# q in PSUM for the attention of a gated layer, GpSimd's sums let run, weight parts handed out by pieces

## The chip, the cores and the metric

The kernel runs on one core of a Trainium2 chip. The metric is the device time of one execution in microseconds. Three runs of the kernel before gave 785.12, 785.23 and 786.01; the median is 785.23.

## The reference

All inputs are float32: S = 2048 positions, D = 640 channels, 32 heads of 20 channels, F = 1536.

```python
xn = _layernorm(x)
# s: attention of each position over 8 earlier ones, 2 apart
qkv = xn @ wqkv                    # D x 3D, split into q, k, v and 32 heads of 20
idx = pos[:, None] - arange(8) * 2 # W, dil = 8, 2
logits = einsum("bhsd,bhswd->bhsw", q, k[idx]) * 20 ** -0.5   # idx < 0: -1e9
o = einsum("bhsw,bhswd->bhsd", softmax(logits), v[idx])
s = o.reshape(B, S, D) @ wo
# g: a gated feed-forward
h = (xn @ w_gate) * (xn @ w_up)    # D x F each
return x + s * silu(h @ w_down)
```

## The kernel before

Every product runs on TensorE as three products of split numbers: each operand is cut into a high part (ScalarE copies it to float32r) and a low part (the rest, subtracted on VectorE or GpSimd), and high x high, high x low and low x high are added up in one PSUM bank (`mm3`, L96). The low part of the weights enters only with the last third of a product.

The program is one long list of instructions. Each engine works through its own list in order, so the order in which the code issues them is the schedule. The stages are:

- layer norm, transposition and the first products (to about 76 us);
- the stage of the units. The attention is cut into 12 units: 6 groups of 5 or 6 heads (`GROUPS`), each for the even and the odd positions. A unit needs 8 `qkv` products (L365); units from the second group on go through a scratch in DRAM and are read back with `load_kq` and `load_kv`. After every two units come two *pieces* `gate_up(f, ch)` (L528): the product of 128 columns of the gate weights, then of the up weights, with 512 positions, 15 matmuls each. ScalarE copies the gate result out of PSUM (`gs`, L539), and VectorE multiplies it with the up result, straight from PSUM (`hs`, L550). That multiplication is put off (`finish_piece`) until the next piece or a later place;
- the rest of the pieces, from 327 us to 565 us; at the end of it the output projection is prepared;
- the output projection in pairs of rows (`pair_product`, L918) and singly, and then the down projection (`product`, L787), both by a scheme with seven products for eight, to the end.

The attention itself is a Python generator (`attention`, L396). `qkv` loops and pieces call `advance` with a budget, and the generator issues VectorE work until the costs it yields have used up the budget. For each unit it goes over four pairs of window places: VectorE multiplies q, read twice, with k shifted (`t`, L445), sums over the 20 channels (`lg`, L463), and in between does the previous unit's values: e times v into one of two buffers (`t` or, for place 0, `o`, L425), which GpSimd adds to `o` (L427). The softmax follows, with the exponential on ScalarE (L485). The e of a unit lies in PSUM.

GpSimd's list is ordered by hand too. A one-element copy of `t` (`behind`, L153) ahead of the sums makes GpSimd wait for the q·k multiplication:

```python
nc.vector.tensor_mul(t, q, k)
if late or beside:
    behind(t[:, 0, :1])
if late:
    late.pop()()
if beside:
    beside.pop(0)[1]()
```

`beside` holds the low parts of the next block of gate and up weights (L143): three subtractions for each block f from 3 to 10, put there by `split_wf_beside(f + 1)` after the block's first piece. What is left of them is issued by `all_beside(f)` ahead of block f's first piece.

PSUM has eight banks: three turn for the tag q (qkv products and most others), two each for g and u (gate and up), one is e.

Of the kernel before, what the change touches and what calls it, by code (L numbers as in the profile page):

```python
# [19 lines left out]
P = 128  # L20
# [7 lines left out]
CH = 512  # L28
# [23 lines left out]
def kernel(  # L52
# [23 lines left out]
    def st(shape, tag, bufs, dt=F32):  # L76
        cnt[0] += 1
        return sb.tile(shape, dt, tag=tag, bufs=bufs, name=f"{tag}_{cnt[0]}")

    def pt(shape, tag, bufs):  # L80
        cnt[0] += 1
        return ps.tile(shape, F32, tag=tag, bufs=bufs, name=f"{tag}_{cnt[0]}")

# [14 lines left out]
    def skip(n):  # L98

        cnt[0] += 1  # L100
        sb.tile([P, n // 4], F32, tag=f"skip_{cnt[0]}", bufs=1, name=f"skip_{cnt[0]}")
# [40 lines left out]
            k = slice(k0, min(k0 + 2, KD))  # L142
            beside.append((f, lambda k=k: nc.gpsimd.tensor_sub(lo[:, k], raw[:, k], hi[:, k].bitcast(F32))))  # L143

    def some_beside(t):

        if beside:
            behind(t[:, 0, :1])
            beside.pop(0)[1]()

    def behind(y):

        nc.gpsimd.tensor_copy(no_wait[0], y)  # L153
# [14 lines left out]
    def load_x(s, n, t, cuts=(0, D)):  # L168
# [3 lines left out]
        for i in range(n):  # L172
            xt[s + i] = t[:, i, :]

    skip(128)
    xa, xe = st([P, 3, D], "t", 2), st([P, 3, D], "t", 2)
    load_x(0, 1, xa[:, 0:1], (0, HALF, D))
# [218 lines left out]
    def attention():  # L396

        def flat(y):
            return y.rearrange("p i c -> p (i c)")

        twice = st([P, 2, NE * CMAX], "t", 2)
        terms = st([P, 2, NE * CMAX], "t", 2)
        weights = pt([P, CH], "e", 1)
        places = NE * W
        m_ps = weights[0:1, CH - places:].rearrange("p (i w) -> p i w", w=W)
        nc.vector.tensor_copy(m_ps, mask)
        before, late, loaded = None, [], set(range(DIL))

        def ahead(n, parts):

            if n < len(ORDER) and ORDER[n] in made:
                for a in parts:
                    if (n, a) not in loaded and ORDER[n] >= DIL:
                        loaded.add((n, a))
                        (load_kq if a == 0 else lambda u: load_kv(u, 1))(ORDER[n])

        def values(w):

            u, e, o = before
            nh = GROUPS[UN[u][0]]  # L420
            c = nh * DH
            y = flat(o)
            t = terms[:, w % 2, :NE * c] if w else y
            v = flat(kv_t[u][:, 1, w:w + NE, :]).rearrange("p (n d) -> p n d", d=DH)
            nc.vector.tensor_mul(t.rearrange("p (n d) -> p n d", d=DH),  # L425
                                 e[:, :, w].unsqueeze(2).to_broadcast([P, NE * nh, DH]), v)
            return NE * c * 1.3e-3, lambda: nc.gpsimd.tensor_add(y, y, t)  # L427

        for n, u in enumerate(ORDER + [None]):
            if u is not None:  # L430
                while u not in made:
                    yield None
                ahead(n, (0, 1))
                g, r = UN[u]
                nh = GROUPS[g]
                c = nh * DH
                q, kv = flat(q_t[u]).unsqueeze(1).to_broadcast([P, 2, NE * c]), kv_t[u]
                lg = st([P, NE * nh, W], "lg", 2)
                t = twice.rearrange("p a c -> p (a c)")[:, :2 * NE * c].rearrange("p (a c) -> p a c", a=2)
            for j in PAIRS:  # L440
                if u is not None:
                    ahead(n + 1, (0,))
                    k = flat(kv[:, 0, j:j + NE, :])
                    k = bass.AP(k.tensor, k.offset, [k.ap[0], [c, 2], k.ap[1]])
                    nc.vector.tensor_mul(t, q, k)  # L445
                    if late or beside:
                        behind(t[:, 0, :1])
                    if late:
                        late.pop()()
                    if beside:  # L450
                        beside.pop(0)[1]()
                    yield 2 * NE * c * 1.22e-3
                elif late:
                    late.pop()()
                if before is not None:
                    cost, add = values(j or 1)
                    if j:
                        add()
                    else:
                        late.append(add)  # L460
                    yield cost
                if u is not None:
                    nc.vector.tensor_reduce(out=lg[:, :, j:j + 2].rearrange("p n a -> p a n"),  # L463
                                            in_=t.rearrange("p a (n d) -> p a n d", d=DH), op=ALU.add, axis=AX.X)
                    yield 2 * NE * c * 1.2e-3
                if before is not None:
                    cost, add = values(j + 1 if j else 0)
                    if j:
                        late.append(add)
                    yield cost  # L470
            if late:
                late.pop()()
            if u is None:
                store_o(before)
                return
            ahead(n + 1, (0, 1))
            m0 = lg[0:1].rearrange("p (i h) w -> p i h w", h=nh)
            nc.vector.tensor_add(m0, m0, m_ps.unsqueeze(2).to_broadcast([1, NE, nh, W]))
            e = weights[:, :NE * nh * W].rearrange("p (n w) -> p n w", w=W)
            most = weights[:, CH - places - NE * nh:CH - places]  # L480
            sm = st([P, 2, NE * nh], "sm", 2)
            nc.vector.tensor_reduce(out=most, in_=lg, op=ALU.max, axis=AX.X)
            nc.vector.tensor_sub(lg, lg, most.unsqueeze(2).to_broadcast([P, NE * nh, W]))
            yield 1.5
            nc.scalar.activation(e, lg, AF.Exp, scale=SCALE)  # L485
            finish_piece()
            yield 0.5
            nc.vector.tensor_reduce(out=sm[:, 0, :], in_=e, op=ALU.add, axis=AX.X)
            nc.vector.reciprocal(sm[:, 1, :], sm[:, 0, :])
            nc.vector.tensor_mul(e, e, sm[:, 1, :].unsqueeze(2).to_broadcast([P, NE * nh, W]))  # L490
            if before is not None:
                store_o(before)
            before = u, e, st([P, NE, c], "o", 1)
            yield 1.3

    def store_o(unit):

        u, _, o = unit
        g, r = UN[u]
        c = GROUPS[g] * DH  # L500
        for b in range(NQ):
            c0, c1 = max(GOFF[g], b * QC), min(GOFF[g] + c, (b + 1) * QC)
            if c0 < c1:
                nc.sync.dma_start(o_scr[r, b, :, :, c0 - b * QC:c1 - b * QC].rearrange("s p c -> p s c"),
                                  o[:, :, c0 - GOFF[g]:c1 - GOFF[g]])
# [3 lines left out]
    def advance(budget):  # L509
        credit[0] += budget  # L510
        while running and credit[0] > 0:
            cost = next(running[0], 0)
            if cost == 0:
                running.pop()
            elif cost is None:
                break
            else:
                credit[0] -= cost
        if credit[0] > 0:
            credit[0] = 0  # L520
# [4 lines left out]
    def gate_up_half(f, ch, n, p, c=slice(0, CH), **parts):  # L525
        mm3(p[:, c], [([t[:, k, n, :] for t in wf[f]], [t[:, k, c] for t in xT[ch]]) for k in range(KD)], **parts)

    def gate_up(f, ch, between=(), amid=(), part=None):  # L528
        if part is None:
            pp = [pt([P, CH], "g", 2), pt([P, CH], "u", 2)]  # L530
            c = slice(0, CH)
        else:
            pp, c = part, slice(CH // 2, CH)
        last = (f, ch) == (KF - 1, NCH - 1)
        gate_up_half(f, ch, 0, pp[0], c)
        for act in amid:
            act()
        gs = st([P, CH], "gs", 2)
        nc.scalar.activation(gs, pp[0], AF.Copy)  # L539
        for act in between:  # L540
            act()
        share = (c.stop - c.start) / CH
        finish_piece()
        advance(PACE * 3.25 * share)
        gate_up_half(f, ch, 1, pp[1], c)

        def finish():
            hs = st([P, CH], "hs", 2)
            if not last:
                nc.vector.tensor_mul(hs, pp[1], gs)  # L550
            else:
                nc.scalar.activation(hs, pp[1], AF.Copy)
                nc.gpsimd.tensor_mul(hs, hs, gs)
            nc.sync.dma_start(h_scr[ch * TPC:(ch + 1) * TPC, :, f, :].rearrange("t p c -> p t c"),
                              hs.rearrange("p (t c) -> p t c", c=P))

        unfinished.append(finish)
        if last:
            finish_piece()
        advance(PACE * 3.25 * share)  # L560

    unfinished = []
# [716 lines left out]
```

## Time and profile before

| | |
|---|---|
| median of three runs | 785.23 us |
| profiled execution: its time | 785.18 us |
| profiled execution: its span in the trace | 783.4 us |
| TensorE busy | 764.4 us (98%) |
| VectorE busy | 611.7 us (78%) |
| ScalarE busy | 234.1 us (30%) |
| GpSimd busy | 293.6 us (37%) |
| mean granted TensorE clock | 0.99 |

The profile names engines PE (TensorE), PEld (its weight loads), DVE (VectorE), ACT (ScalarE), POOL (GpSimd) and SP (SyncE, which issues the DMAs). A row of groups gives line, engine, operation, output and inputs with shapes and count, then busy microseconds and the mean nanoseconds of one, then the idle time before them and what ended it. A row of the timeline gives start and duration in microseconds and in brackets the idle time before it with its releaser. A row of the waits gives the waiting engine and line, what it waited for, the total, the count and the longest. The chain that ended last is given in order of time: start, duration, engine, tile, line. A row of stretches gives the stretch and its length, the busy time of PE, PEld, DVE, ACT and POOL, the granted clock, and the DMA's share and GB/s.

### The profile page before, as it was taken

To read this page: it belongs to the slowest core of one execution; us is meant where nothing else is said; L and a number is where in the kernel's file an instruction comes from. 1 tells how busy PE (TensorE), PEld (TensorE's weight loads), DVE (VectorE), ACT (ScalarE), POOL (GpSimd) and SP (SyncE) were. 2 spreads that over 40 slices of the span, in tenths; PEclk is the share of its full clock that TensorE was granted. 3 is DMA by queue.
4 is the path that set the end of the run, shared out by engine and by line. 5 is a ranking of instruction groups with operands and counts; after the bars stand their busy time and mean duration, and the time that the engine had idled before them with its cause. 6 is when DMAs were issued, how large, how long until landed. Compare 5 with 4: busy or idle time off the path is not lost.

```text
span 783.4 us, 11385 instructions
## 1 busy us (share of the span) xinstructions
PE 764.4 (98%) x4402; PEld 702.6 (90%) x4402; DVE 611.7 (78%) x749; ACT 234.1 (30%) x459; POOL 293.6 (37%) x247
## 2 busy tenths in 40 slices
PE   8998999999999999999999879999999999999997
PEld 6988899998989989988878658888899999999997
DVE  7898897999999999899999501113788977777775
ACT  4323212222222212111011011021465664444442
POOL 5200262653646644744657650102547920000000
PEclk9999999999999999999999979999999999999999
DMA  9561227465464735566332232254268574555523
GB/s 321 169 197 54 64 77 250 137 212 166 134 214 137 244 112 158 181 177 177 98 113 74 52 86 74 74 147 119 95 182 252 200 262 158 190 197 182 182 101 134
DMA packets 93634, 120.54 MB, mean 154 GB/s; under 512 B 23976, under 2 KB 68384, under 8 KB 93452
## 3 DMA queue, kind: packets, MB, share of 16 engines
q1 hardware_dynamic: 93580, 119.82, 48.8%
q8 instruction: 34, 0.56, 0.3%
q14 instruction: 20, 0.16, 0.1%
HBM read 76.79 MB, written 41.58 MB: 151 GB/s over the span
## 4 chain that ended last, share of the span: by engine, by line
PE 88%; DVE 7%; POOL 2%; DMA 1%; issue 1%; ACT 1%; SPq 0%; POOLq 0%; DVEq 0%; ACTq 0%
PE q L374 25%; PE u L96 18%; PE g L96 17%; PE q L787 11%; PE u L787 5%; PE q L96 3%; PE q L918 3%; PE g L787 3%; POOL o L427 2%; PE u L918 1%; DVE xc L250 1%; DVE ot L313 1%; PE g L918 1%; DVE t L445 1%; DVE stats L222 1%
## 5 line engine op out<-in xcount | busy, mean ns | idle before, releaser
L96 PE MATMUL g<-xc,wf 128*128 128x512 f32 (+1 forms) x735 | 173.8, 387 | 9.9 <-POOL wf L143 9.9
L427 POOL TENSOR_TENSOR o<-o,t 128x800 f32<-128x800 f32 (+1 forms) x84 | 170.7, 2032 | 13.2 <-DVE o L425 7.0
L96 PE MATMUL u<-xc,wf 128*128 128x512 f32 (+1 forms) x735 | 173.4, 388 | 0.0
L96 PEld LDWEIGHTS g<-xc,wf 128*128 128x128 f32 x735 | 136.1, 189 | 38.4 <-POOL wf L143 11.8
L96 PEld LDWEIGHTS u<-xc,wf 128*128 128x128 f32 x735 | 137.2, 190 | 27.9
L374 PE MATMUL q<-wqh,xc 128*128 128x300 f32 (+1 forms) x960 | 158.7, 309 | 2.9 <-ACT q L388 2.9
L374 PEld LDWEIGHTS q<-wqh,xc 128*128 128x128 f32 x960 | 144.8, 189 | 4.9 <-ACT q L388 3.4
L445 DVE TENSOR_TENSOR t<-q,kv 128x1600 f32<-128x1600 f32 (+1 forms) x48 | 107.1, 2231 | 0.1
L550 DVE TENSOR_TENSOR hs<-u,gs 128x512 f32<-128x512 f32 x47 | 32.0, 681 | 79.9 <-PE u L96 63.0
L539 ACT ACTIVATE gs<-g 128x512 f32<-128x512 f32 x48 | 28.7, 599 | 212.6 <-PE g L96 188.3
L463 DVE TENSOR_REDUCE lg<-t 128x80 f32<-128x1600 f32 (+1 forms) x48 | 92.1, 1920 | 0.1
L425 DVE TENSOR_TENSOR t<-e,kv 128x800 f32<-128x800 f32 (+1 forms) x84 | 87.0, 1036 | 5.5 <-POOL o L427 5.4
L374 PE MATMUL q<-wql,xc 128*128 128x300 f32 (+1 forms) x480 | 86.0, 308 | 0.1
L381 ACT ACTIVATE ot<-q 128x300 f32<-128x300 f32 (+1 forms) x80 | 35.4, 442 | 145.9 <-PE q L374 136.9
L374 PEld LDWEIGHTS q<-wql,xc 128*128 128x128 f32 x480 | 74.2, 189 | 0.4 <-DVE wql L87 0.3
L787 PE MATMUL q<-xc,wf 128*128 128x320 f32 x432 | 67.3, 309 | 0.0
L787 PEld LDWEIGHTS q<-xc,wf 128*128 128x128 f32 x432 | 64.3, 188 | 0.0
L153 POOL COPY beside<-t 128x1 f32<-128x1 f32 x38 | 7.0, 185 | 147.3 <-DVE t L445 142.8
L143 POOL TENSOR_TENSOR wf<-wraw,wf 128x512 fp32r<-128x512 f32 (+1 forms) x24 | 26.3, 1108 | 28.3 <-ACT wf L139 28.3
L87 POOL TENSOR_TENSOR xc<-wraw,xc 128x320 fp32r<-128x320 f32 (+1 forms) x22 | 27.1, 1237 | 18.3 <-ACT xc L86 18.3
L87 POOL TENSOR_TENSOR wql<-wraw,wqh 128x300 fp32r<-128x300 f32 (+2 forms) x6 | 8.6, 1440 | 60.8 <-ACT wqh L86 60.8
L87 POOL TENSOR_TENSOR wf<-wraw,wf 128x256 fp32r<-128x256 f32 (+2 forms) x13 | 13.8, 1088 | 25.0 <-ACT wf L86 25.0
(266 smaller groups left out, 933.8 us busy)
## 6 DMA issues: line engine op xcount, KB each, us to landing
h_scr<-hs SPq DMA_DIRECT2D x48, 256.0 KB, 2.2
wraw<-in_wgu SPq DMA_DIRECT2D x12, 640.0 KB, 4.8
qkv_scr<-ot SPq DMA_DIRECT2D x12, 600.0 KB, 3.5
t<-h_scr SPq DMA_DIRECT2D x8, 768.0 KB, 6.6
hs<-s_scr SPq DMA_DIRECT2D x16, 320.0 KB, 3.6
gs<-in_x SPq DMA_DIRECT2D x16, 320.0 KB, 4.3
kv<-qkv_scr SPq DMA_DIRECT2D x12, 400.0 KB, 4.7
out<-q SPq DMA_DIRECT2D x14, 320.0 KB, 2.5
```

Of the source, the lines that this page charges most:

```text
L87: eng.tensor_sub(lo, raw, hi.bitcast(F32))
L96: nc.tensor.matmul(acc, a, b, start=first and n == 0, stop=last and n == len(runs) - 1)
L374: nc.tensor.matmul(p, xT[(r * NE + i) // TPC][a][:, k, t0:t0 + P], wq[g][b][:, k], start=n == 0, stop=n == len(runs) - 1, skip_group_check ...
L381: nc.scalar.activation(staged[u][:, :, i - i0, :], p.rearrange("p (a c) -> p a c", a=3), AF.Copy)
L425: nc.vector.tensor_mul(t.rearrange("p (n d) -> p n d", d=DH), e[:, :, w].unsqueeze(2).to_broadcast([P, NE * nh, DH]), v)
L427: return NE * c * 1.3e-3, lambda: nc.gpsimd.tensor_add(y, y, t)
L445: nc.vector.tensor_mul(t, q, k)
L463: nc.vector.tensor_reduce(out=lg[:, :, j:j + 2].rearrange("p n a -> p a n"), in_=t.rearrange("p a (n d) -> p a n d", d=DH), op=ALU.add, ax ...
L539: nc.scalar.activation(gs, pp[0], AF.Copy)
L550: nc.vector.tensor_mul(hs, pp[1], gs)
L787: nc.tensor.matmul(p, y[:, i, k], wd_t[name][k][:, l], start=new and r == 0, stop=r == len(runs) - 1, skip_group_check=True)
L918: nc.tensor.matmul(b, y, w, start=new and r == 0, stop=r == len(runs) - 1, skip_group_check=True)
```

## The change

- The three banks of q become `q_one` (one bank) and `q_two` (two banks in one tile). A ring hands them out in turn to whatever asks for the tag q. While the attention runs, the ring is `q_one`, the next bank of g, the next bank of u, and `q_two` holds the q of the unit in attention: ScalarE copies it there from SBUF at the start of each unit, and L445 reads it from PSUM.
- The one-element copies ahead of GpSimd's sums in the attention are gone, and each sum is issued right after its product, except the one of the first pair, which is issued after the product of place 0 that it adds to.
- `beside` is no longer emptied in the attention but in `gate_up`: one low part ahead of the up product and one after it.
- A unit that was not ready when the attention came to it would leave five further turns empty after its loads are issued.

```diff
+    ring, turns = [], [0]
+    def part(y, shape):
+        n = math.prod(shape[1:])
+        y = y[:, :n]
...
     def pt(shape, tag, bufs):
+        if tag == "q":
+            turns[0] += 1
+            y = ring[turns[0] % len(ring)]
+            if isinstance(y, str):
+                return pt(shape, y, 2)
+            return part(y, shape)
         cnt[0] += 1
         return ps.tile(shape, F32, tag=tag, bufs=bufs, name=f"{tag}_{cnt[0]}")
...
-    def some_beside(t):
-
+    def some_beside():
         if beside:
-            behind(t[:, 0, :1])
             beside.pop(0)[1]()
...
+    q_one, q_two = pt([P, CH], "q1", 1), pt([P, 2 * CH], "q2", 1)
+    three = [q_one, q_two[:, :CH], q_two[:, CH:]]
+    ring += three
...
+        ring[:] = [q_one, "g", "u"]
         for n, u in enumerate(ORDER + [None]):
             if u is not None:
+                late_unit = u not in made
                 while u not in made:
                     yield None
                 ahead(n, (0, 1))
+                for _ in range(5 if late_unit else 0):
+                    yield None
                 g, r = UN[u]
                 nh = GROUPS[g]
                 c = nh * DH
-                q, kv = flat(q_t[u]).unsqueeze(1).to_broadcast([P, 2, NE * c]), kv_t[u]
+                nc.scalar.activation(q_two[:, :NE * c], flat(q_t[u]), AF.Copy)
+                q, kv = q_two[:, :NE * c].unsqueeze(1).to_broadcast([P, 2, NE * c]), kv_t[u]
...
                     nc.vector.tensor_mul(t, q, k)
-                    if late or beside:
-                        behind(t[:, 0, :1])
-                    if late:
-                        late.pop()()
-                    if beside:
-                        beside.pop(0)[1]()
                     yield 2 * NE * c * 1.22e-3
-                elif late:
-                    late.pop()()
...
                     cost, add = values(j + 1 if j else 0)
                     if j:
-                        late.append(add)
+                        add()
+                    else:
+                        late.pop()()
                     yield cost
-            if late:
-                late.pop()()
             if u is None:
                 store_o(before)
+                ring[:] = three
                 return
...
         finish_piece()
         advance(PACE * 3.25 * share)
+        some_beside()
         gate_up_half(f, ch, 1, pp[1], c)
...
         if last:
             finish_piece()
+        some_beside()
         advance(PACE * 3.25 * share)
```

More of the change, by code (lines that the diff above doesn't have):

```diff
@@ L78, in st @@
         return sb.tile(shape, dt, tag=tag, bufs=bufs, name=f"{tag}_{cnt[0]}")
-    def pt(shape, tag, bufs):
+    ring, turns = [], [0]
+    def part(y, shape):
+        n = math.prod(shape[1:])
+        y = y[:, :n]
+        if len(shape) == 3:
+            return y.rearrange("p (a b) -> p a b", b=shape[2])
+        if len(shape) == 4:
+            return y.rearrange("p (a b c) -> p a b c", b=shape[2], c=shape[3])
+        return y
+    def pt(shape, tag, bufs):
+        if tag == "q":
[4 more added lines that the diff above has]
+            return part(y, shape)
         cnt[0] += 1
```

## The prediction

> **What bounds the kernel now.** I read the page first, then who waited for whom, then the chain that ended last.
>
> ```profile
> span 783.4 us, 11385 instructions
> PE 764.4 (98%) x4402; PEld 702.6 (90%) x4402; DVE 611.7 (78%) x749; ACT 234.1 (30%) x459; POOL 293.6 (37%) x247
> PE g L96 <- POOL wf L143: 9.9, 2, 8.3
> POOL beside L153 <- DVE t L445: 142.8, 35, 14.7
> ```
>
> TensorE is busy 98% of the span, so a change to GpSimd, ScalarE or VectorE can gain only what TensorE idles because of them. The largest such wait is 9.9 us in two pieces: a gate product waits for GpSimd's low part of its weights (L143). The 142.8 us for which GpSimd is held back by the one-element copies (L153) is not TensorE's time.
>
> The chain, in order of time, says what those two waits cost with all that follows them. From 327.28 us to the pair products TensorE does nothing but gate/up pieces: 33 of them by the code (25 of the 32 of the middle weight blocks, since 7 were used between the units, and 4 for each of the last two).
>
> ```profile
> 327.28 3.40 PE g L96 x15
> 393.76 3.42 PE u L96 x15
> 456.61 1.65 PE g L96 x3
> 458.26 4.88 PE u L96 x15
> 463.14 3.41 PE g L96 x15
> 561.75 3.40 PE u L96 x15
> 440.00:460.00 20.00, 11.66 (x42) 8.70 (x41) 6.98 (x7) 1.20 (x2) 16.77 (x10) 0.77 0.28 77
> ```
>
> An undisturbed half lasts 3.40 us, so 66 halves should take 224.4 us. They take 561.75 + 3.40 - 327.28 = 237.87. The stretch loses 13.45 us: the 9.9 of waiting, and 3.5 of slow products behind the longer wait (4.88 instead of 3.40, at a granted clock of 0.77 in that slice, the last row). Between the start of attention and 327.28 the chain is TensorE without a gap. So 13.45 us is all that can be gained.
>
> **The two stalls.** The timeline around them:
>
> ```profile
> 392.48 0.73 POOL L143 TENSOR_TENSOR wf<-wraw,wf 128x256 fp32r<-128x256 f32 x1
> 393.26 0.50 PE L96 MATMUL g<-xc,wf 128*128 128x512 f32 x1 [1.53 <-POOL wf L143]
> 436.68 1.16 DVE L425 TENSOR_TENSOR o<-e,kv 128x960 f32<-128x960 f32 x1 [1.91 <-DMA o_scr<-o]
> 437.97 16.13 POOL L427 TENSOR_TENSOR o<-o,t 128x960 f32<-128x960 f32 x7 [6.98 <-DVE o L425]
> 444.62 2.43 PE L96 MATMUL g<-xc,wf 128*128 128x512 f32 x10
> 446.01 0.68 DVE L550 TENSOR_TENSOR hs<-u,gs 128x512 f32<-128x512 f32 x1
> 454.06 3.18 POOL L143 TENSOR_TENSOR wf<-wraw,wf 128x512 fp32r<-128x512 f32 x3
> 455.37 2.88 PE L96 MATMUL g<-xc,wf 128*128 128x512 f32 x5 [8.33 <-POOL wf L143]
> ```
>
> Before, a low part is handed out only with a q·k multiplication of attention. The last unit had none left when the weights of block 8 came, so all three low parts went out at the block's first piece, behind the seven sums of the last unit (16.13 us). TensorE did its ten products with high parts and then waited 8.33 us.
>
> **Part 1, low parts handed out by pieces.** Two go out in the second piece of the block before and the third in the middle of the third piece. For block 8 the first two then stand ahead of the last unit's sums and the third behind two of them: it starts at about 436.4 + 2 x 2.3 = 441 and ends at 441.7. It is wanted by the eleventh product, at 444.78 + 2.27 - 1.6 (the first stall is gone) = 445.5. For block 6, whose third part ended at 393.2, the hand-out moves about two pieces (some 13 us) up. Both stalls go, with the slow products: -13.45 us. What is late next at 446 is the up product of the same piece. Its bank is free when the DVE has done the multiplication hs of two pieces earlier, which ended at 446.69 and whose VectorE predecessors go at the pace of the sums. The third low part inside that row of sums adds 0.73, the earlier TensorE takes away 1.0 to 1.6: 445.8 to 446.4. The product wants it at 444.78 + 3.40 - 1.6 = 446.6. So 0 is expected, with a margin of 0.2 to 0.8 us; were the DVE a whole half (3.40) later, about 3 us would come back. The gap before that was 1.53 us and was followed by a half of 3.42, so a short stall costs its own length only.
>
> **Part 2, q copied to PSUM.**
>
> ```profile
> L445 DVE TENSOR_TENSOR t<-q,kv 128x1600 f32<-128x1600 f32 x32 | 67.6, 2113 | 0.1
> L445 DVE TENSOR_TENSOR t<-q,kv 128x1920 f32<-128x1920 f32 x16 | 39.5, 2468 | 0.0
> L445 DVE TENSOR_TENSOR t<-q,kv x48: 1803/2148/3475, 76.0 to 421.1; 128x1600 f32<-128x1600 f32 x32, 128x1920 f32<-128x1920 f32 x16
> 399.43 2.15 DVE L445 TENSOR_TENSOR t<-q,kv 128x1920 f32<-128x1920 f32 x1
> 385.80 2.27 POOL L427 TENSOR_TENSOR o<-o,t 128x960 f32<-128x960 f32 x1
> 386.82 3.26 DVE L445 TENSOR_TENSOR t<-q,kv 128x1920 f32<-128x1920 f32 x1
> 390.28 2.25 POOL L427 TENSOR_TENSOR o<-o,t 128x960 f32<-128x960 f32 x1
> 391.67 2.14 DVE L463 TENSOR_REDUCE lg<-t 128x96 f32<-128x1920 f32 x1
> L425 DVE TENSOR_TENSOR t<-e,kv 128x800 f32<-128x800 f32 x56 | 54.8, 979 | 0.0
> L739 DVE TENSOR_TENSOR wql<-t,wqh 128x768 f32<-128x768 f32 x4 | 3.8, 951 | 0.0
> ```
>
> The q·k multiplication has both inputs in SBUF. It takes 2.15 us alone, but 3.26 when a GpSimd sum is running: it ends 2.0 us after the sum, as if it had waited for it. The reduction, with one input, takes 2.14 beside a sum, no longer than the multiplication alone, and L425, whose e lies in PSUM already, takes 979 ns in the mean of 56, what its elements cost by the slope worked out below. With q in PSUM I expect L445 to behave like L425: 32 x (2113 - 1803) + 16 x (2468 - 2150) = 15.0 us of VectorE time saved. None of it is TensorE's, so it counts as nothing in the sum, but it pays for delays below. 800 elements with e in PSUM take 979 ns and 768 from SBUF 951: the difference is what 32 elements cost (1.03 ns each, from 979 for 800 and 1803 for 1600), so the place costs nothing extra. The Trainium skill's Perfetto Trace Analysis (Optimizing Scalar/DVE Operations) speaks against that: it puts a DVE instruction's fixed cost at about 60 ns on SBUF and about 125 on PSUM. By it an estimated 48 x 65 ns = 3 us of the DVE's 15 would go, and the sum would stand. The two rows disagree with the page.
>
> The copies themselves: 12, one for each unit, on ScalarE.
>
> ```profile
> L746 ACT ACTIVATE wf<-wqh 128x768 fp32r<-128x768 f32 x16 | 13.5, 846 | 20.1 <-PE g L787 10.0 <-PE q L787 8.9 <-DVE wqh L734 1.0
> L485 ACT ACTIVATE e<-lg 128x384 f32<-128x384 f32 x4 | 2.0, 494 | 7.1 <-DVE lg L483 7.1
> 76.05 1.80 DVE L445 TENSOR_TENSOR t<-q,kv 128x1600 f32<-128x1600 f32 x1
> 78.20 0.25 ACT L388 ACTIVATE q<-q 128x100 f32<-128x100 f32 x1
> 83.33 0.68 DVE L550 TENSOR_TENSOR hs<-u,gs 128x512 f32<-128x512 f32 x1
> 87.48 3.40 PE u L96 x15
> 363.71 2.47 DVE L445 TENSOR_TENSOR t<-q,kv 128x1920 f32<-128x1920 f32 x1
> 364.81 0.60 ACT L539 ACTIVATE gs<-g 128x512 f32<-128x512 f32 x1 [2.68 <-PE g L96]
> ```
>
> 494 ns for 384 elements into PSUM (the exponential) and 846 for 768 into SBUF give 0.87 us for 800 and 1.02 for 960; half or double of it moves the margins by half a microsecond. ScalarE is busy 30%, so the 11 us cost nothing there. But the copy adds a wait: the unit's first multiplication waits for it, behind it on the DVE stand the reductions and the hs multiplications that free the u banks, and ahead of it on ScalarE stands what was issued before, possibly an evacuation waiting for TensorE. For the first unit it stands behind the row at 78.20, so the multiplication starts at 78.45 + 0.87 = 79.3, not 76.05, and hs moves from 83.33 to 86.6, ending at 87.3. For unit 9 it stands behind the row at 364.81 and moves 363.71 to 366.4 (+2.7), and unit 11 likewise; for the others the copy runs while the DVE does the softmax's last three small steps. All this is below the 15 us saved. The five empty turns for a unit that isn't ready cost nothing: by the planner's costs every unit is ready when attention comes to it.
>
> **Part 3, sums not held back.** 38 copies of 185 ns leave GpSimd. The sums start when their products are there, about one q·k multiplication (2.15 us) earlier than now. They are off TensorE's path: 0.
>
> **Part 4, the banks.** Of eight PSUM banks three served q, two g, two u, one e. Now q of the unit has two, and the qkv products turn through one own bank and the g and u banks. Within a unit they still come round after three products. What is new is that a qkv product right after two pieces takes a u bank, which the DVE must have freed, and that the first piece of attention needs hs of the piece before it: u at 87.48 wants what I just placed at 87.3. Counting turns, u comes first in the stage that starts at 190.48, and there the second u bank is wanted by the fourth product, at 190.48 + 3 x 2.05 = 196.6 (2.05 is the stage's 32.80 over 16 products, row below).
>
> ```profile
> 190.48 32.80 PE q L374 x240
> 174.16 2.95 DVE L445 TENSOR_TENSOR t<-q,kv 128x1600 f32<-128x1600 f32 x1
> 197.44 0.68 DVE L550 TENSOR_TENSOR hs<-u,gs 128x512 f32<-128x512 f32 x1
> ```
>
> As things stand the DVE frees it at 198.12, 1.5 us late. The multiplication at 174.16 loses 1.15 us to a sum, which comes back, so 0 to 0.4 is left, and 1.5 at most. In the stages at 97.68, 144.08, 236.88 and 288.88 u comes second or third and the like count leaves 2 us or more. I add 0.5 us for all such waits (bounds: 0 and 3).
>
> **The sum.** 785.18 (the profiled execution; its span 783.4 and 1.8 around it, and the median is 785.23) - 13.45 + 0.5 = 772.2, say 772.3. Ends of the likeliest case: 771.6 with no new wait; 775 with 3 us of them.
>
> **Rivals.**
> Given back in part: the DVE, late from copies that wait behind evacuations, frees u banks late, at 446 and at two or three of the stages. 3.4 us, one half, at each of one to three places: 775 to 782. For it speak the margins of 0.2 to 0.8 us; against it the 15 us that the DVE saves.
>
> Slower: the shared u banks stall TensorE at the start of all five qkv stages. This decides when the DVE is some 5 us later than now at each, so that hs misses both u banks, each by over 1.5 us: five times 3.4 = 17, 785.2 - 13.4 + 17 = 789. It would come if L445 with q in PSUM is no faster, or if ScalarE's queue holds the copy for a whole product chain each time. Against it: only one of the ten bank returns is tight by the count above. The Trainium skill's Perfetto Trace Analysis (Matmul Optimizations) asks that all eight banks be used for parallel work, and parking two of them under q goes against it; the trace bears that page out only at 196.6.
>
> It doesn't do what it says: the sums and the low part of block 8 still end in the same order, only the first stall goes: 785.2 - 1.5 = 783.7; and within 1.6 us if neither goes. Against it: the hand-out is in the code, ahead of the last unit's values.
>
> **The numbers.** Likeliest case (771 to 775) 0.70; given back in part, 775 to 783.6, 0.17; no difference, 0.02; slower 0.11. A measurement of this kernel can tell about 0.2%, 1.6 us, from no change. Faster 0.87, same 0.02, slower 0.11. The range reaches from 770.9 into the second case, to 779.
>
> **What would show it.** Right: no TensorE wait on L143 in the gate/up stretch, 66 halves in about 224.4 us, L445 at about 1.81 and 2.15 us with little spread, the granted clock at 1.0 around 450. Wrong: idle time of TensorE released by DVE hs, at 87, 197, 446 or at the starts of the qkv stages; L445 above 2.1; a DVE idle before L445 of over 3 us for each copy.

## The result, and the profile after

The changed kernel takes 795.36 us (median of 4 runs, 793.46 to 795.39); the kernel before, beside it, 785.17. The ratio is 1.0127 (95% interval 1.0104 to 1.015): 10.2 us slower, where 13 us faster was forecast.

The first lines of the page after, and TensorE's waits (waiting engine and line, releaser, total, count, longest):

```profile
span 793.6 us, 11374 instructions
PE 767.1 (97%) x4402; PEld 706.3 (89%) x4402; DVE 597.5 (75%) x749; ACT 244.4 (31%) x471; POOL 287.9 (36%) x211
...
PE q L393 <- ACT q L407: 11.1, 4, 4.2
PE q L806 <- ACT q L787: 3.9, 3, 1.3
PE q L213 <- POOL ident masks.py:199: 1.4, 1, 1.4
PE q L393 <- DVE xc L294: 1.3, 1, 1.3
PE q L114 <- ACT gs L668: 1.2, 2, 0.7
PE q L393 <- DVE rstd L251: 1.2, 1, 1.2
```

and before, the only wait for a reader of the tag q:

```profile
PE q L374 <- ACT q L388: 2.9, 2, 2.4
```

(The lines have moved: L374 is now L393, L96 L114, L445 L469, L427 L446, L550 L568, L787 L806, L918 L937, and ScalarE's reads of a qkv product, L387 and L388, are L406 and L407. L787 is now ScalarE's read of q in the down projection, L668 and L940 are its reads in the output projection.) The wait for GpSimd's low parts is gone. In its place stand waits for readers of the tag q, ScalarE above all. They are not where attention runs: between 84 and 567 us TensorE waits for nothing. The chain that ended last:

```profile
14.65 3.87 PE q L393 x15
29.46 4.12 PE q L393 x15
76.21 8.08 PE q L393 x45
...
342.54 3.40 PE g L114 x15
...
563.53 3.40 PE u L114 x15
566.93 0.88 PE q L937 x6
...
652.46 2.65 PE q L806 x18
656.41 2.91 PE q L806 x18
```

Three differences add up. The gate/up stretch now starts at 342.54 instead of 327.28: 15.26 us lost before it. It ends at 566.93, so its 66 halves take 224.39 us instead of 237.87: 13.48 won. From there to the end of the span it is 793.6 - 566.93 = 226.67 instead of 783.4 - 565.15 = 218.25: 8.42 lost. 15.26 - 13.48 + 8.42 = 10.2, the whole difference of the spans.

The first of the three lies ahead of the piece that starts at 69.06 before and at 84.29 now. Up to it TensorE does the same 365 matmuls (first row before, second row after):

```profile
0.00:69.06 69.06, 64.39 (x365) 56.41 (x366) 59.32 (x174) 26.07 (x71) 15.83 (x43) 0.98 0.62 210
0.00:84.29 84.29, 68.71 (x365) 61.59 (x366) 59.34 (x174) 26.84 (x71) 15.74 (x43) 0.90 0.51 172
```

It idles 15.6 us instead of 4.7, which is 10.9 more, and the same matmuls take 4.3 us longer, at a mean granted clock of 0.90 instead of 0.98.

What a lost place looks like, in the timeline at 29 us, in the layer-norm stage:

```profile
28.75 0.30 ACT L248 ACTIVATE rstd<-mvo,eps 128x4 f32<-128x4 f32 x1 [3.33 <-DVE mvo L242]
28.95 0.32 ACT L406 ACTIVATE kv<-q 128x200 f32<-128x200 f32 x1
29.17 0.24 ACT L407 ACTIVATE q<-q 128x100 f32<-128x100 f32 x1
29.46 1.62 PE L393 MATMUL q<-wqh,xc 128*128 128x300 f32 x5 [4.17 <-ACT q L407]
```

A qkv product waits 4.17 us until ScalarE has read the qkv product just before it, from another bank. ScalarE is late with that because its list holds a square root ahead of it (L248) that waits 3.33 us for VectorE. In the kernel before ScalarE was as late, but the second product did not wait for it:

```profile
20.45 1.53 PE L374 MATMUL q<-wqh,xc 128*128 128x300 f32 x10
24.79 0.30 ACT L229 ACTIVATE rstd<-mvo,eps 128x4 f32<-128x4 f32 x1 [3.34 <-DVE mvo L223]
25.21 0.25 ACT L388 ACTIVATE q<-q 128x100 f32<-128x100 f32 x1
```

The ten matmuls at 20.45 are the last five of one qkv product and the first five of the next, which went into the next bank of the tag some 4 us before L388 read the first. The delay is handed on: at 38.39 VectorE waits 8.04 us for ScalarE's copy of a later product (L324), where it waited 0.98 before. The granted clock from 0 to 40 us was 0.83, where it was 1.00. At 656.41 the same sign stands in the down projection, and again at 713.43 and 770.44: each time 1.31 us, once in each round of the ring (each group of seven products takes one q bank there, so a round is three groups).

The theory that this gave (A): `q_two` is one tile, and the program orders uses of its two halves as if they were one place. Where the ring goes from the first half to the second, the product waits for the reader of the product just before it, although the banks differ. The rivals were that parking two banks and copying q costs the time (B), and that a bank kept in one tile all through, instead of being given back and taken anew, costs it (C).

### The profile page after: what moved, and what is told of

It reads as the page before. It is cut to its first block, busy times and chain, and to the rows that moved or that the text cites. A ratio compares the mean times of both kernels' runs of the same rounds, so it can differ in the third digit from the quotient of the medians.

```text
span 793.6 us, 11374 instructions
## 1 busy us (share of the span) xinstructions
PE 767.1 (97%) x4402; PEld 706.3 (89%) x4402; DVE 597.5 (75%) x749; ACT 244.4 (31%) x471; POOL 287.9 (36%) x211
## 4 chain that ended last, share of the span: by engine, by line
PE 91%; DVE 6%; ACT 1%; issue 1%; DMA 1%; SPq 0%; ACTq 0%; DVEq 0%
PE g L114 19%; PE u L114 19%; PE q L806 11%; PE q L393 10%; PE g L393 8%; PE u L393 7%; PE u L806 5%; PE q L114 3%; PE g L806 3%; PE q L937 3%; PE u L937 1%; DVE stats L241 1%; DVE xc L269 1%; DVE ot L332 1%; PE g L937 1%
## 5 line engine op out<-in xcount | busy, mean ns | idle before, releaser
L446 POOL TENSOR_TENSOR o<-o,t 128x800 f32<-128x800 f32 (+1 forms) x84 | 172.6, 2055 | 155.3 <-DVE o L444 94.4
L114 PE MATMUL g<-xc,wf 128*128 128x512 f32 (+1 forms) x735 | 172.6, 387 | 0.0
L114 PE MATMUL u<-xc,wf 128*128 128x512 f32 (+1 forms) x735 | 171.8, 385 | 0.0
L114 PEld LDWEIGHTS g<-xc,wf 128*128 128x128 f32 x735 | 136.7, 190 | 26.9
L114 PEld LDWEIGHTS u<-xc,wf 128*128 128x128 f32 x735 | 136.0, 188 | 27.4
L469 DVE TENSOR_TENSOR t<-q,kv 128x1600 f32<-128x1600 f32 (+1 forms) x48 | 92.4, 1925 | 12.8 <-ACT q L460 11.0
L393 PE MATMUL q<-wqh,xc 128*128 128x300 f32 (+1 forms) x410 | 76.4, 320 | 13.6 <-ACT q L407 11.1
L568 DVE TENSOR_TENSOR hs<-u,gs 128x512 f32<-128x512 f32 x47 | 32.0, 682 | 67.9 <-PE u L114 50.2
L393 PEld LDWEIGHTS q<-wqh,xc 128*128 128x128 f32 x410 | 66.2, 200 | 15.4 <-ACT q L407 12.0
L806 PE MATMUL q<-xc,wf 128*128 128x320 f32 x432 | 67.6, 310 | 3.9 <-ACT q L787 3.9
L806 PEld LDWEIGHTS q<-xc,wf 128*128 128x128 f32 x432 | 64.2, 188 | 4.7 <-ACT q L787 4.7
L393 PE MATMUL g<-wqh,xc 128*128 128x300 f32 (+1 forms) x280 | 49.9, 308 | 0.0
L393 PE MATMUL u<-wqh,xc 128*128 128x300 f32 (+1 forms) x270 | 48.0, 307 | 0.0
L393 PEld LDWEIGHTS g<-wqh,xc 128*128 128x128 f32 x280 | 43.2, 188 | 0.2
L393 PEld LDWEIGHTS u<-wqh,xc 128*128 128x128 f32 x270 | 41.6, 188 | 0.1
L393 PE MATMUL q<-wql,xc 128*128 128x300 f32 (+1 forms) x205 | 38.3, 318 | 0.0
L393 PEld LDWEIGHTS q<-wql,xc 128*128 128x128 f32 x205 | 33.3, 200 | 0.0
```

The source lines that it names most:

```text
L114: nc.tensor.matmul(acc, a, b, start=first and n == 0, stop=last and n == len(runs) - 1)
L393: nc.tensor.matmul(p, xT[(r * NE + i) // TPC][a][:, k, t0:t0 + P], wq[g][b][:, k], start=n == 0, stop=n == len(runs) - 1, skip_group_check ...
L806: nc.tensor.matmul(p, y[:, i, k], wd_t[name][k][:, l], start=new and r == 0, stop=r == len(runs) - 1, skip_group_check=True)
```

## The experiments

**The ring alone, with halves of one tile.** The kernel before, with nothing of the change but the ring, all through:

```diff
+        if tag == "q":
+            turns[0] += 1
+            return part(ring[turns[0] % len(ring)], shape)
...
+    q_one, q_two = pt([P, CH], "q1", 1), pt([P, 2 * CH], "q2", 1)
+    ring += [q_one, q_two[:, :CH], q_two[:, CH:]]
```

> The kernel before, with nothing changed but the three q banks: they are handed out in turn from q_one and the two halves of q_two, as the changed kernel does outside the attention, and here all through. Theory A (the two halves of one tile are ordered as one: a product into the second half waits until the reader of the first half is done): the first 97 us lose about 15 us and the last 218 us about 8.4, as in the changed kernel, and in the qkv stages every third product waits some 0.7 us, 27 times, so about 19 more; the two waits for L143 stay. About 785 + 15 + 8 + 19 = 827, between 808 and 835. Theory B (the loss comes from something else in the change, such as the two banks parked under q or the copies): 785 within 2 us.

831.79 us, ratio 1.0602 (1.0586 to 1.0618). TensorE's waits (L391 is the qkv product; L398, L405 and L785 are ScalarE's reads of tag q for the later units, the first group and the down projection):

```profile
PE q L391 <- ACT ot L398: 13.6, 25, 0.6
PE q L391 <- ACT q L405: 11.6, 5, 4.2
PE g L111 <- POOL wf L158: 9.5, 2, 8.4
PE q L804 <- ACT q L785: 3.9, 3, 1.3
```

and the timeline in a qkv stage:

```profile
117.19 0.42 ACT L398 ACTIVATE ot<-q 128x300 f32<-128x300 f32 x1 [1.63 <-PE q L391]
117.67 0.95 PE L391 MATMUL q<-wqh,xc 128*128 128x300 f32 x5 [0.51 <-ACT ot L398]
...
119.17 1.56 PE L391 MATMUL q<-wqh,xc 128*128 128x300 f32 x10
120.06 0.42 ACT L398 ACTIVATE ot<-q 128x300 f32<-128x300 f32 x1 [2.45 <-PE q L391]
```

No q in PSUM, no copy, no freed sums, and yet 47.6 us slower. In the qkv stages there are 25 waits of 0.54 us in the mean, for about a third of the 80 products, and the stages last 23.8 us longer in all, since the three products behind a wait are slower, too (6.58 us for 6.15); the waits on L785 are the changed kernel's, to the tenth. From the first pair product, at 603.49, to the end of its span of 830.1 it takes 226.6 us, the changed kernel's 226.67 again. The 47.6 is the sum expected of A with the qkv stages dearer than guessed (23.8 us for 19). B falls.

**The ring alone, with three tiles.**

```diff
-    q_one, q_two = pt([P, CH], "q1", 1), pt([P, 2 * CH], "q2", 1)
-    ring += [q_one, q_two[:, :CH], q_two[:, CH:]]
+    ring += [pt([P, CH], tag, 1) for tag in ("q1", "q2", "q3")]
```

> The same ring as in the run with halves of one tile, but of three tiles of one bank each. Theory A (one tile, ordered as one): no loss, 785 within 1.5 us. Theory C (a bank that is kept in one tile all through, and not given back and taken anew, costs the waits): as slow as with the halves, over 800.

784.23 us against 784.20, ratio 1.0005 (0.9994 to 1.0015). The same ring, the same order, and nothing lost: C falls. The two runs differ only in whether two of the banks belong to one tile. That is the cause of the loss outside the attention.

**The changed kernel with two tiles for q.** The copy and the q·k multiplication are cut in two, one half for each bank:

```diff
-    q_one, q_two = pt([P, CH], "q1", 1), pt([P, 2 * CH], "q2", 1)
-    three = [q_one, q_two[:, :CH], q_two[:, CH:]]
+    three = [pt([P, CH], tag, 1) for tag in ("q1", "q2", "q3")]
+    q_one, q_two = three[0], three[1:]
...
+                for b in range(2):
+                    nc.scalar.activation(q_two[b][:, :hc], flat(q_t[u])[:, b * hc:(b + 1) * hc], AF.Copy)
...
+                    for b in range(2):
+                        k = flat(kv[:, 0, j:j + NE, :])[:, b * hc:(b + 1) * hc]
+                        k = bass.AP(k.tensor, k.offset, [k.ap[0], [c, 2], k.ap[1]])
+                        nc.vector.tensor_mul(t[:, :, b * hc:(b + 1) * hc],
+                                             q_two[b][:, :hc].unsqueeze(1).to_broadcast([P, 2, hc]), k)
```

> The changed kernel with q_two as two tiles of one bank; q of a unit is copied half into each, and the q.k multiplication is done in two halves (400 or 480 elements of each copy of q), some 48 x 0.15 = 7 us more of VectorE. Theory A: start and end are as before the change and the gate/up stretch is without a stall: 785.2 - 13.4 = 771.8, at most 774. Theory B: as the changed kernel, 793 to 796.

771.87 us, ratio 0.9835 (0.9818 to 0.9852). The q·k multiplications take 95.5 us in two halves, 3 more than in one piece. The chain: the stretch from 325.94 to 550.34 is 224.40 us, and from there to the end of the span of 768.6 it is 218.26, as before the change.

```profile
325.94 3.40 PE g L114 x15
...
546.94 3.40 PE u L114 x15
550.34 0.88 PE q L940 x6
```

By the medians that is 12.3 us less than the kernel before beside it (784.20), where the prediction had 12.9. The profiled execution is the shortest of the four (770.38): it gains another 1.34 us ahead of the stretch, where the granted clock from 60 to 80 us was 1.00 instead of 0.91. The run with the sums held, below, shows 0.91 there again, as before the change, so this is not counted to the change. With two tiles the change is worth what the prediction said. Which part of it is worth that?

**The hand-out alone.** The kernel before with `some_beside` in `gate_up` and out of the attention:

```diff
-                    if late or beside:
-                        behind(t[:, 0, :1])
                     if late:
+                        behind(t[:, 0, :1])
                         late.pop()()
-                    if beside:
-                        beside.pop(0)[1]()
...
         advance(PACE * 3.25 * share)
+        some_beside()
         gate_up_half(f, ch, 1, pp[1], c)
...
+        some_beside()
         advance(PACE * 3.25 * share)
```

> The kernel before with one part of the change only: the low parts are handed out in the pieces, ahead of the up product and after it; q stays in SBUF, the sums stay held back, the banks turn as before. If the hand-out alone takes the two stalls away (the prediction's part 1): 771.8, at most 773. If the sums must run free or q must be in PSUM for it: between 774 and 785, with a wait of TensorE for L143 or for VectorE left near 392 or 447.

773.92 us, ratio 0.9868 (0.985 to 0.9885): between the two in time, and with the sign of the second. Both waits for low parts are gone, which is worth 10.3 us; a wait for VectorE's hs has come, at the place where the prediction left a margin of 0.2 to 0.8 us. Timeline (L425 is the sum, L423 the values, L546 hs):

```profile
430.87 2.24 POOL L425 TENSOR_TENSOR o<-o,t 128x960 f32<-128x960 f32 x1
437.08 1.16 DVE L423 TENSOR_TENSOR o<-e,kv 128x960 f32<-128x960 f32 x1 [2.78 <-DMA o_scr<-o]
442.94 0.74 POOL L143 TENSOR_TENSOR wf<-wraw,wf 128x256 fp32r<-128x256 f32 x1
447.00 0.68 DVE L546 TENSOR_TENSOR hs<-u,gs 128x512 f32<-128x512 f32 x1
447.74 3.74 PE L96 MATMUL u<-xc,wf 128*128 128x512 f32 x15 [1.77 <-DVE hs L546]
```

The last sum of unit 9, put off behind two low parts, ends at 433.1; its store, the next unit's first product into o (437.08, before 436.68) and all seven sums follow, with the third low part among them, and hs ends at 447.68, before 446.69.

**The hand-out, and the sums let run; q stays in SBUF.**

```diff
-                    if late:
-                        behind(t[:, 0, :1])
-                        late.pop()()
                     yield 2 * NE * c * 1.22e-3
-                elif late:
-                    late.pop()()
...
                     if j:
-                        late.append(add)
+                        add()
+                    else:
+                        late.pop()()
                     yield cost
-            if late:
-                late.pop()()
```

> The run with the hand-out alone, and besides it GpSimd's sums let run, while q stays in SBUF. Theory A with contention (a multiplication with two SBUF inputs stands still while a GpSimd sum runs): L445 grows beyond the 2.11 and 2.47 us of before, to 2.6 and 3.0 or more in the mean (about 25 us more of VectorE), hs comes later, and TensorE waits for hs at 447 longer than the 1.8 us of the run with the hand-out alone: 775 to 785. Rival: it is the hold-back that made hs late there; then 771.8 and no wait for hs.

771.29 us, ratio 0.9836 (0.982 to 0.9852), and no wait for hs. The theory with contention missed, the rival held. Groups of sums and multiplications by shape (count, then busy us and mean ns):

```profile
L425 POOL TENSOR_TENSOR o<-o,t 128x800 f32<-128x800 f32 x56 | 138.2, 2468 | 80.1 <-DVE o L423 53.6 <-DVE t L423 24.1
L425 POOL TENSOR_TENSOR o<-o,t 128x960 f32<-128x960 f32 x28 | 78.6, 2807 | 26.7 <-DVE o L423 24.0 <-DVE t L423 1.4
L443 DVE TENSOR_TENSOR t<-q,kv 128x1600 f32<-128x1600 f32 x32 | 64.7, 2020 | 0.1
L443 DVE TENSOR_TENSOR t<-q,kv 128x1920 f32<-128x1920 f32 x16 | 40.7, 2541 | 0.0
```

They do contend, but it is mostly GpSimd that pays: 2468 and 2807 ns for a sum, where with q in two PSUM tiles it was 1947 and 2263, while the multiplication stays at 105.3 us in all, against 107.1 before the change. GpSimd, at 44% of the span, can pay. Here hs of that place ends at 444.48 and its up product starts at 445.01: 0.5 us left.

**Two tiles, with the sums held back.** The run with two tiles, with the lines above put back.

> The run with two one-bank tiles, but with the sums held back by the one-element copies as before the change. If letting the sums run is off TensorE's path (the prediction's part 3): 771.9 within 1 us, L445's halves as short as there. Rival: the held sums bring the store of o and with it hs of 444 later than the 0.7 us that are left there: 772.5 to 775 with a TensorE wait for hs.

771.73 us, ratio 0.9839 (0.9824 to 0.9854): as with the sums free, and without a wait for hs: hs of that place ends at 445.72, and its product starts at 445.98, so 0.3 us are left of the 0.7.

**Two tiles, with the hand-out as before.** In the run with two tiles `some_beside()` leaves `gate_up` and stands behind the q·k multiplication.

> The run with two one-bank tiles, but the low parts are handed out with the q.k multiplications as before the change (without the one-element copies). If the two stalls come from the hand-out (the prediction's part 1): the long wait at 447 stays, since the last unit has no multiplications left, 8 us with the slow products behind it, and the short one at 392 shrinks or goes: 782 to 785. Rival: with q in PSUM and the sums free GpSimd is early enough anyway: 772 to 775.

782.06 us, ratio 0.9975 (0.9964 to 0.9987). TensorE's longest wait:

```profile
PE g L114 <- POOL wf L161: 8.4, 1, 8.4
```

The short stall goes, the long one stays, as part 1 had it. So q in PSUM and free sums together are worth 1.9 us without the hand-out, and the hand-out is worth 10 on top of them (782.06 - 771.87).

The ratio is to the kernel before, run beside each (784.20 us for the first four, 783.94 for the others):

| kernel | us | ratio |
|---|---|---|
| ring of halves alone | 831.79 | 1.0602 |
| ring of three tiles alone | 784.23 | 1.0005 |
| the change, q in two tiles | 771.87 | 0.9835 |
| hand-out alone | 773.92 | 0.9868 |
| hand-out, sums free, q in SBUF | 771.29 | 0.9836 |
| the change, q in two tiles, sums held | 771.73 | 0.9839 |
| the change, q in two tiles, old hand-out | 782.06 | 0.9975 |

Five of these beat both kernels, four of them by over 1%. The shortest of these edits to 771 us is the hand-out with the sums let run, without any q in PSUM.

## Why the prediction was wrong, point by point

- *What bounds the kernel, and the 13.45 us:* right. The stretch is 13.48 us shorter in the changed kernel, and its granted clock is 1.00 all through, where it was 0.98. (From the rows the sum is 237.87 - 224.4 = 13.47, and the lower end without a new wait 771.7, not 771.6.)
- *Part 1, the hand-out:* right for the two stalls, which go in the changed kernel and in the hand-out alone; the long one stays without the hand-out (782.06). Its margin for hs came out by luck. The part counts with the hand-out alone, takes 1.0 to 1.6 us off for the earlier TensorE and has 0.2 to 0.8 us left. With the hand-out alone hs came 1.0 us later than before, not earlier: VectorE waits there for GpSimd's sums and not for TensorE, and 1.77 us were missing. With the whole change 0.72 us are left (hs done at 460.65, the product at 461.37; the same with two tiles, 444.06 and 444.78). That comes from the sums let run or from q in PSUM, either of which is enough (0.5 and 0.3 us left), and which the prediction put at nothing for TensorE.
- *Part 2, q in PSUM:* the terms were right and the conclusion too. L469 took 1814 and 2148 ns (expected 1810 and 2150), 92.4 us in all instead of 107.1: 14.7 saved for 15.0 forecast. With q in PSUM the multiplication of 1600 elements takes 11 ns more in the mean than the shortest with both inputs in SBUF (1803 ns), and that of 1920 none (2148 against 2.15 us alone). The Trainium skill's Perfetto Trace Analysis (Optimizing Scalar/DVE Operations), with its about 60 ns for SBUF and 125 for PSUM, would make it an estimated 65 ns; these rows do not agree with it:

```profile
L469 DVE TENSOR_TENSOR t<-q,kv 128x1600 f32<-128x1600 f32 x32 | 58.1, 1814 | 5.9 <-ACT q L460 4.2 <-DMA kv<-qkv_scr 1.7
L469 DVE TENSOR_TENSOR t<-q,kv 128x1920 f32<-128x1920 f32 x16 | 34.4, 2148 | 6.8 <-ACT q L460 6.8
L460 ACT ACTIVATE q<-q 128x800 f32<-128x800 f32 x8 | 6.7, 833 | 0.0
L460 ACT ACTIVATE q<-q 128x960 f32<-128x960 f32 x4 | 3.9, 969 | 0.0
```

  The copies took 0.83 and 0.97 us (0.87 and 1.02), and VectorE waited 11.0 us for them, five times.
- *Part 3, the sums:* nothing of TensorE's, right where q is in PSUM (771.73 held, 771.87 free). With q in SBUF holding them back costs the 1.77 us at 447, and some 2.5 in all (773.92 to 771.29). 36 of the 38 copies left, not all: two stand in the layer-norm stage.
- *Part 4, the banks:* here it failed. The part counts who shares banks while the attention runs, and finds one tight return, at 196.6. None of those waits came: TensorE waits for nothing from 84 to 567 us in the changed kernel, and the 0.5 us put in for it was 0. But the part took for granted that the ring outside the attention, one own bank and two halves of a tile, does what three banks of the tag q did. It opened no row of the first 97 us or of the last 218 for this, and the sum has no term for them. The trace of the changed kernel puts 15.26 and 8.42 us there, and the runs with rings of halves and of three tiles show why: a product into the second half waits for the reader of the first, and with three tiles nothing is lost.
- *The rivals:* the slower one (789 us, 0.11) had the banks, but the wrong ones and the wrong stage: u banks returned late by VectorE at the five qkv stages. The trace shows q halves ordered as one, where no attention runs. No rival asked what the change does to code that it only hands other buffers to.

## What to carry to other kernels

When a change replaces what buffers come from, go through every place that takes one, not only those that the change is about, and ask for each: what does the next user now wait for? Two buffers made as parts of one tile may be ordered as one; a wait on a reader that isn't the buffer's own, once per round of the ring, is its sign. And take a bundle of edits apart before judging it: here one edit carried most of the gain (10.3 of 12.3 us) and another, which wasn't needed for it, all the loss. An edit that is worth nothing in one combination can still hold up a margin in another, so a margin is counted for the whole change.

## What was not expected of the hardware

Where a GpSimd sum and a VectorE multiplication with two SBUF inputs overlapped, these rows show the one that began first running on and the other standing still until it had ended. In the run with the hand-out and the sums let run:

```profile
371.70 2.15 DVE L443 TENSOR_TENSOR t<-q,kv 128x1920 f32<-128x1920 f32 x1
371.92 4.06 POOL L425 TENSOR_TENSOR o<-o,t 128x960 f32<-128x960 f32 x1 [9.37 <-DVE o L423]
```

The multiplication took the 2.15 us that it takes alone. The sum began 0.22 us after it and ended 2.1 us after it, about its own length with q in PSUM (2.26). In the kernel before it was the other way round: the sums, held until a multiplication had ended, ran into the next one, which took 3.26 us. So the order decides who pays. With the sums held they took 1919 and 2259 ns in the mean (56 of 800 elements, 28 of 960), no more than with q in PSUM, and the multiplications bore all of it. With the sums let run they took 2468 and 2807, and the multiplications lost no more in all than before (105.3 us for 107.1).

A wait of 0.54 us for the wrong reader cost nearly twice that in the qkv stages of the ring of halves (23.8 us for 25 waits), at a granted clock of 1.00; why the products behind it were slower stays open. In the layer-norm stage, where ScalarE's list had other work ahead of the read, one such wait was up to 4.2 us long.
